# A fused attention, MLP and mixture-of-experts kernel: one more expert's first layer in fp32r, two loads moved, one wait dropped, new priorities

## The chip, the cores and the metric

The kernel runs on one core of a Trainium2 chip. A core has a matrix engine (TensorE, here PE, with a separate lane PEld for loading weights), three engines for element-wise work (VectorE: DVE, ScalarE: ACT, GpSimd: POOL), a SyncE (SP) that here only issues DMAs, and 16 DMA engines. Each engine runs its own list of instructions in order and waits on semaphores. The metric is the device time in microseconds (us) of one execution. Lower is better.

## The reference

Three layers, one behind the other, all in fp32 as seen from outside:

```python
# q, k, v: (2, 8, 768, 64); proj: (64, 6)
q_bits = np.einsum('bhsd,dk->bhsk', q, proj) > 0        # k_bits likewise
q_bucket = sum(q_bits * 2**arange(6))                    # k_bucket likewise
scores = where(q_bucket == k_bucket, q @ k.T / sqrt(64), -1e9)
x = softmax(scores) @ v                                  # -> (1536, 512)
x = maximum(x @ w_in, 0)**2 @ w_out                      # w_in (512, 2048)
logits = x @ w_gate                                      # 8 experts
for idx in argsort(-logits.flatten()):                   # greedy, best first
    tok, e = divmod(idx, 8)
    if not assigned[tok] and counts[e] < 192: assign(tok, e)
for e in range(8):                                       # w1 (512, 1024), w2 (1024, 512)
    out[mask[e]] = maximum(x[mask[e]] @ w1[e], 0) @ w2[e]
```

Every expert ends with exactly 192 tokens. Which token goes where depends on the order of all 12,288 logits.

## The kernel before

The kernel is written as a set of operations, each with an engine, a duration in a table, what it needs, the buffers it takes and gives back, and a priority. A small list scheduler (`Sched`) plays them through when the program is built and writes each engine's instructions in the order that comes out. On the chip that order is fixed; what varies is only how long each instruction waits. The priorities stand in tables: PREP, PREP1 and PR for attention, MP for the MLP, EP and RP for the router, FP for the experts. A change of a number there changes the order on all engines.

**Attention** has 16 heads, taken in pairs (0 to 7), and 96 units u of 128 queries. `first` prepares head 0 on its own: DVE and ACT copy the loaded k and q (L340, L342), PE transposes them (L355), ACT writes an upper part in fp32r (L360, L363), for q a second copy of it (L366), and DVE the lower part (L371, L374). PE then forms bucket bits (L384 and on). `second` does the same for head 1, `pair` for the later pairs; copies between SBUF partitions go by DMA from SP (L259, 14 for a pair). For each unit PE multiplies scores (L671), DVE takes the maximum (L687), ACT the exp (L690), POOL divides (L699), PE transposes the result (L707), ACT and DVE split it into upper and lower part (L715, L719) and PE multiplies it by v (L728, L729).

**The MLP** converts its weights on ACT and DVE (L870 to L878), splits them into upper and lower parts (ACT L884, POOL L886) and runs its first layer (L896) in the remaining gaps of attention and then by itself; the second layer is L923. The gate weights are loaded at L837, first thing after head 1's loads.

**The router** takes the logits of twelve token tiles. `early` compares all logits of a token (L1282 maximum, L1322 and L1343 comparisons on DVE), PE counts (L1362, L1364), and for each expert phase the router picks the next full expert and its tokens (L1453 comparisons, L1461 counts, and on to L1593, the token numbers). Its constants (`rck`) are loaded at L1148, ahead of everything else on SP, and read for the first time after attention. The routers of the later phases run beside the experts, on DVE above all.

**The experts** run in eight phases p, in the order that the router finds, each in four groups g of 256 hidden units. For a phase, SP reads the expert's number from SBUF and issues the weight loads of group 0 (L1739, L1740); POOL gathers the 192 token rows by two indirect DMAs (L1782) and then copies the number again (L1787), which lets SP issue the loads of groups 1 to 3; PE transposes the tokens (L1799), ACT and DVE bring them to SBUF (L1804, L1806, L1811, L1813). For p below `XP` the first layer is plain fp32 (L1893: eight multiplications of 192 columns a group), and ACT and DVE split the result into upper and lower part straight from PSUM (L1904, L1907). From `XP` on it runs in fp32r: the weights are split first (L1750 on ACT for the upper part, L1752 for the lower part, on POOL for even phases below 7), the upper weights are multiplied with both token parts side by side (L1851, 384 columns), the lower weights with the upper token part (L1852, 192 columns), and four steps form the result's two parts (L1860, L1863 on ACT, L1865, L1868 on DVE). The second layer is L1964 to L1971, its eviction L2027 to L2031, and POOL scatters the rows to the output (L2018).

Of the kernel before, what the change touches and what calls it, by code (L numbers as in the profile page):

```python
# [233 lines left out]
XC = -13  # L234
PREP, PW, DL = -224, 0.8, 2.4
PREP1 = 9.5
LDP = (2, 0)
PR = {"S": -6, "mx": 1033.5, "ex": 915, "dn": 242.5, "rec": -2168, "nrm": 581, "tp": -0.5, "hi": 240, "lo": -1372.5, "pv": 2, "oa": 1474, "od": 631.5, "pe": -246.5, "pa": 548.5, "pd": -695.5}

# [13 lines left out]
def attention(nc, S, ps, mem, ident, q, k, v, proj, pat, xhi, xlo):  # L253
# [9 lines left out]
    pf = mem(AT_PW + .5, [3, 32], R)  # L263
# [59 lines left out]
    def first(cm):  # L323
# [23 lines left out]
        def on(k):  # L347
            return "S" if k in FS else "B"
# [58 lines left out]
        for nm, hf in (("k", 0), ("q", 0), ("k", 1), ("q", 1)):  # L407
# [4 lines left out]
            if hf == 0:  # L412
                T["ci", nm, (0, 0)] = b
            c = add("ACT", .38, lambda hf=hf: hi2(hf), [a, b]) if nm == "q" else None
            d = add("DVE", .47, lambda nm=nm, hf=hf: lo(nm, hf), [a, b, c], rel=[(on("ft"), a)])
            H[nm, hf] = [x for x in (b, c, d) if x is not None]
        S.add("NONE", 0.0, None, [T["ft", "q", 1], T["ft", "k", 1]], rel=[("Pn", T["fl"])])
        out, o, early = [], None, None
        for x, hf in (("qk", 0), ("k", 1), ("q", 1)):
# [7 lines left out]
            if x == "k":  # L427
                early = list(out)
        return early, out

# [378 lines left out]
LEAST = 3.0517578125e-05  # L809
MP = {"lw": -1109, "ac": -526.5, "h1": 594, "h2": 869.5, "ch": -1952, "cv": 82, "sp": -784, "lg": -129, "ev": -2530, "lv": 292, "c0": 4755, "c1": 6377, "b0": -1565, "b1": 1274}  # L810


def mlp(nc, S, ps, mem, ident, xhi, xlo, w_in, w_out, w_gate, wgt, x2d, L, att):
# [22 lines left out]
    sw = S.add("NONE", 0.0, f1, last, rel=[(r, (3000 + u,)) for r, us in dict(r=(14,), xt=(35,)).items() for u in us])  # L836
    wgl = S.add("SP", .62, lambda: nc.sync.dma_start(wg, w_gate.rearrange("(c p) e -> p c e", p=128)), prio=MB)  # L837
    wgl = S.add("DMA", .1, None, [wgl], lat=1.8)
# [262 lines left out]

EP = {"fr": 1831, "lr": -1863.5, "row": -1595, "col": 240.5, "cp": 2055.5, "ca": 20, "gp": 1115}
LONE = 2
# [6 lines left out]
ND = 4  # L1110
RP = {"fr": 2209, "se": 1249, "oh": -1149, "G": 534, "A": -1001.5, "lr": -1816.5, "pf": -2980, "id": -1672, "gp": -626.5, "sq": 1082, "G1": -962, "A1": 813, "ei": -1561.5, "up": -1135.5}
ACT_TILES = {12: (10, 11), 9: (8,), 6: ()}
# [19 lines left out]
class Router:  # L1132
# [31 lines left out]

    def smalls(self, S, deps):
        k, P = self.k, self.nc.gpsimd
        alive, tok = self.alive, self.tok

# [919 lines left out]
def whole(tc, q, k, v, proj, w_in, w_out, w_gate, w1, w2, wgt, pat, rc, out):  # L2088
    nc = tc.nc
    with ExitStack() as ctx, tc.manual_schedule():  # L2090
# [58 lines left out]
```

## Time and profile before

| what | us |
| --- | --- |
| median of three timed runs | 759.81 (757.88 to 760.62) |
| the profiled execution | 757.53 |
| its span, first to last instruction | 755.7 |
| PE busy in the span | 740.3 (98%) |
| DVE busy | 562.8 (74%) |
| ACT busy | 454.9 (60%) |
| POOL busy | 328.5 (43%) |

The trace is one execution; its times count from the start of the span. A busy PE includes matmuls that overlap, so a sum of durations can be more than the time they took. In a row of the timeline, the bracket at the end is the idle time of that engine just before the instruction and what ended it. Attention lies from the start to about 240 us, the MLP up to about 540, the experts from about 560 to the end.

### The profile page before, as it was taken

The numbers are of one execution on the slowest core, as the hardware profiler recorded it, in microseconds if no ns is written. First come the engines' busy times: TensorE is split into PE (matmuls) and PEld (weight loads), VectorE is DVE, ScalarE is ACT, GpSimd is POOL, SyncE is SP. The second block draws the span as 40 slices with busy tenths as digits, with TensorE's granted clock in tenths as the row PEclk, the third lists the DMA queues.
The fourth block names the chain that finished last, engine by engine and source line by source line (L and its number), as shares of the span: only waits on it lengthen the run. The fifth ranks groups of instructions, "written<-read, shape, count | busy, mean of one in ns | idle before, by whom it ended". The sixth has DMA issues, their size and how long they took to land.

```text
span 755.7 us, 13988 instructions
## 1 busy us (share of the span) xinstructions
PE 740.3 (98%) x4955; PEld 652.8 (86%) x4955; DVE 562.8 (74%) x1213; ACT 454.9 (60%) x902; POOL 328.5 (43%) x362
## 2 busy tenths in 40 slices
PE   8999999999999999999999999999999999999996
PEld 5788988988988899998999999898768888888885
DVE  6899999999999876613853783236898978888883
ACT  7999999999998665533342433224453543345772
POOL 3788778778797775633100000004721121223521
PEclk9999999999999999999999999999899999999999
DMA  9879669575721122500330110021156467479921
GB/s 191 185 137 191 133 120 188 119 154 119 172 60 57 68 101 73 172 35 1 112 112 0 57 56 1 0 84 43 44 184 219 154 219 234 135 243 322 312 69 35
DMA packets 77109, 92.76 MB, mean 123 GB/s; under 512 B 29520, under 2 KB 56528, under 8 KB 77040
## 3 DMA queue, kind: packets, MB, share of 16 engines
q1 hardware_dynamic: 74992, 85.58, 41.5%
q0 software_dynamic: 2048, 6.29, 2.8%
q8 instruction: 39, 0.64, 0.4%
q14 instruction: 30, 0.25, 0.1%
HBM read 63.55 MB, written 6.29 MB: 92 GB/s over the span
## 4 chain that ended last, share of the span: by engine, by line
PE 76%; DVE 11%; ACT 4%; issue 3%; DMA 2%; POOL 2%; SPq 0%; POOLq 0%; ACTq 0%; DVEq 0%
PE psTP L896 17%; PE psS L923 12%; PE psS L1893 6%; DVE p L719 5%; PE psS L671 4%; PE psm L923 3%; PE psO L923 3%; DVE f L687 3%; PE psTP L707 2%; PE psO L707 2%; PE psS L1964 2%; PE psS L1968 2%; PE psS L1965 2%; PE psS L1971 2%; PE psS L1966 2%
## 5 line engine op out<-in xcount | busy, mean ns | idle before, releaser
L699 POOL TENSOR_TENSOR f<-f 128x768 f32<-128x768 f32 x96 | 141.7, 1478 | 24.8 <-PE psTP L707 7.9
L896 PE MATMUL psTP<-r 128*128 128x384 f32 x756 | 138.0, 336 | 0.0
L896 PEld LDWEIGHTS psTP<-r 128*128 128x128 f32 x756 | 132.3, 188 | 2.4 <-POOL r L886 0.2
L905 DVE TENSOR_TENSOR f<-f,psTP 128x384 f32<-128x384 f32 x63 | 34.9, 554 | 88.2 <-ACT f L903 88.1
L923 PE MATMUL psS<-r 128*128 128x512 f32 x384 | 100.3, 395 | 0.0
L687 DVE TENSOR_REDUCE f<-psS 128x1 f32<-128x768 f32 x96 | 90.6, 943 | 0.7 <-PE psS L671 0.5
L690 ACT ACTIVATE f<-psS,f 128x768 f32<-128x768 f32 x96 | 87.0, 906 | 5.4 <-POOL f L699 2.6
L671 PE MATMUL psS<-r 128*128 128x384 f32 x384 | 87.5, 349 | 1.7 <-ACT f L690 1.4
L903 ACT ACTIVATE f<-psTP 128x384 f32<-128x384 f32 x63 | 31.0, 492 | 86.0 <-PE psTP L896 85.9
L923 PEld LDWEIGHTS psS<-r 128*128 128x128 f32 x384 | 70.8, 188 | 12.7
L671 PEld LDWEIGHTS psS<-r 128*128 128x128 f32 x384 | 65.6, 188 | 5.3 <-ACT f L690 4.2
L1322 POOL TENSOR_SCALAR f<-f,mx 128x768 bf16<-128x768 f32 (+1 forms) x3 | 8.0, 2675 | 141.9 <-ACT f L1308 134.8
L1893 PE MATMUL psS<-ff,rf 128*128 128x192 f32 x320 | 60.4, 331 | 0.3 <-DVE ff L1813 0.3
L1750 ACT ACTIVATE ff<-rf 128x1024 fp32r<-128x1024 f32 x32 | 33.8, 1056 | 34.5 <-PE psS L1966 23.7
L1893 PEld LDWEIGHTS psS<-ff,rf 128*128 128x128 f32 x320 | 52.1, 190 | 2.4 <-DVE ff L1813 0.6
L907 ACT ACTIVATE r<-f 128x384 fp32r<-128x384 f32 x64 | 33.5, 524 | 32.0 <-DVE f L905 32.0
L2018 POOL DMA_INDIRECT out_dram<-ff,ix x16 | 17.6, 1102 | 80.6 <-DVE ff L2029 41.4
L719 DVE TENSOR_TENSOR p<-psTP,p 128x384 fp32r<-128x384 f32 x86 | 47.1, 549 | 5.4 <-ACT p L715 3.3
L909 POOL TENSOR_TENSOR r<-f,r 128x384 fp32r<-128x384 f32 x28 | 33.1, 1185 | 37.5 <-ACT r L907 29.2
L1782 POOL DMA_INDIRECT ff<-x2d,ix x16 | 18.2, 1137 | 66.1 <-DVE ix L1593 38.7
L728 PE MATMUL psTP<-p,r 128*128 128x384 f32 x114 | 46.4, 407 | 0.5 <-DVE p L719 0.5
L715 ACT ACTIVATE p<-psTP 128x384 fp32r<-128x384 f32 x86 | 42.4, 496 | 5.0 <-PE psTP L707 4.3
(422 smaller groups left out, 1797.9 us busy)
## 6 DMA issues: line engine op xcount, KB each, us to landing
rf<-in_moe_w_dram SPq DMA_DIRECT2D x64, 512.0 KB, 7.0
r<-r SPq DMA_DIRECT2D x84, 192.0 KB, 4.1
f<-in_moe_w_in_dram SPq DMA_DIRECT2D x16, 512.0 KB, 3.9
f<-in_moe_w_out_dram SPq DMA_DIRECT2D x16, 512.0 KB, 4.8
r<-r SPq DMA_DIRECT2D x14, 384.0 KB, 3.9
f<-in_k_dram SPq DMA_DIRECT2D x8, 384.0 KB, 6.4
f<-in_q_dram SPq DMA_DIRECT2D x8, 384.0 KB, 5.8
f<-in_v_dram SPq DMA_DIRECT2D x8, 384.0 KB, 4.8
```

Of the source, the lines that this page charges most:

```text
L671: nc.tensor.matmul(sbank(u)[:, hf, 0:384], T["q", (pr, h)][:, n, 128 * i:128 * i + 128], T["k", (pr, h)][:, n, 384 * hf:384 * hf + 384], s ...
L687: nc.vector.tensor_reduce(col(0, u), sbank(u)[:, :, 0:384], axis=AX.XY, op=OP.max, negate=True)
L690: nc.scalar.activation(P(u).rearrange("p (a b) -> p a b", a=2), sbank(u)[:, :, 0:384], AF.Exp, bias=col(0, u), accum_out=col(1, u))
L699: nc.gpsimd.tensor_tensor(Pn(u), P(u), col(3, u).to_broadcast([128, 768]), op=OP.mult)
L715: nc.scalar.activation(th, tp(u, g), AF.Copy)
L719: nc.vector.tensor_tensor(tl, tp(u, g), th.bitcast(F32), op=OP.subtract)
L728: nc.tensor.matmul(obank(g), w, th[:, c], start=(c == 0), stop=False)
L896: nc.tensor.matmul(hbank(s, hf), w[:, c], y[:, x, sl], start=(c == 0 and i == 0), stop=(c == 3 and i == 2))
L905: nc.vector.tensor_tensor(r, r, hbank(s, hf), op=OP.mult)
L923: nc.tensor.matmul(abank(i), a[:, t], w, start=(f == RUNS[r][1][0] and j == 0), stop=(f == RUNS[r][1][-1] and j == 2))
L1750: nc.scalar.activation(h(p, g, 0), w, AF.Copy)
L1893: nc.tensor.matmul(abank(n)[:, j], raw(p, g)[:, 0, 256 * c + 128 * j:256 * c + 128 * j + 128], xT(p)[:, c], start=(c == 0), stop=(c == 3))
```

## The change

Four things, in code that is otherwise the same. Line numbers grow by 3 from about L418 and by 5 from about L1170.

1. `XP` goes from 5 to 4: the fifth expert's first layer runs in fp32r too. Its phase is even, so its lower weight parts are formed on POOL.
2. The load of the router's constants moves from the start of the program into `smalls`, where it waits for the score matmul of unit 29 (`att[4][4]`); the load of the gate weights waits for that of unit 35 (`sos[5]`).
3. In `first`, the lower part of q no longer waits for q's second copy, which is now an operation of its own.
4. The priority tables have new numbers.

```diff
-PREP, PW, DL = -224, 0.8, 2.4
-PREP1 = 9.5
+PREP, PW, DL = -167, 0.8, 2.4
+PREP1 = 9
-PR = {"S": -6, "mx": 1033.5, "ex": 915, ...
+PR = {"S": -7, "mx": 1911, "ex": 835.5, ...
@@ first
-        ld, H = {}, {}
+        ld, H, H2 = {}, {}, []
...
-            c = add("ACT", .38, lambda hf=hf: hi2(hf), [a, b]) if nm == "q" else None
-            d = add("DVE", .47, lambda nm=nm, hf=hf: lo(nm, hf), [a, b, c], rel=[(on("ft"), a)])
-            H[nm, hf] = [x for x in (b, c, d) if x is not None]
+            d = add("DVE", .47, lambda nm=nm, hf=hf: lo(nm, hf), [a, b], rel=[(on("ft"), a)] if nm == "k" else ())
+            H[nm, hf] = [b, d]
+            if nm == "q":
+                c = S.add("ACT", .38, lambda hf=hf: hi2(hf), [a, b], prio=-99.5)
+                S.add("NONE", 0.0, None, [c, d], rel=[(on("ft"), a)])
+                H2.append(c)
...
-                early = list(out)
-        return early, out
+                early = [*out, H2[0]]
+        return early, [*out, *H2]
@@ mlp
-    wgl = S.add("SP", .62, lambda: nc.sync.dma_start(wg, ...), prio=MB)
+    wgl = S.add("SP", .62, lambda: nc.sync.dma_start(wg, ...), [sos[5]], prio=MB)
@@ Router
-        nc.sync.dma_start(k, rc)
+        self.rc = rc
...
+        a = S.add("SP", .62, lambda: self.nc.sync.dma_start(k, self.rc), begun, prio=MB)
+        deps = [*deps, S.add("DMA", .6, None, [a], lat=1.8)]
@@ experts
-HP, XP = 0, 5
+HP, XP = 0, 4
```

The order of the instructions, at the places where it matters. First SP at the start of the program; the names are the tile written and the tensor read. Before:

```order
L1148 DMA rck<-in_rc_dram 128x301
L334 DMA f_118<-in_k_dram 128x384
L334 DMA f_118<-in_q_dram 128x384
L275 DMA f_118<-in_proj_dram 64x6
L276 DMA f_118<-in_proj_dram 64x6
```

Now, the same place:

```order
L334 DMA f_117<-in_k_dram 128x384
L334 DMA f_117<-in_q_dram 128x384
L275 DMA f_117<-in_proj_dram 64x6
L276 DMA f_117<-in_proj_dram 64x6
L277 DMA f_117<-in_pat_dram 32x512
```

The two moved loads now stand some pairs further on, each among the copies (L259) that SP issues for a pair, the constants ahead of the last two copies of one pair and the gate weights within those of the next:

```order
L1170 DMA rck<-in_rc_dram 128x301
L259 DMA r_113<-r_113 64x768 x2
L538 DMA f_117<-in_v_dram 128x2x384
L540 DMA f_117<-in_q_dram 128x12x64
L540 DMA f_117<-in_k_dram 128x12x64
L259 DMA r_113<-r_113 64x2x768
L259 DMA r_113<-r_113 64x768
L840 DMA f_117<-in_moe_w_gate_dram 128x4x8
L259 DMA r_113<-r_113 64x768 x5
```

Five copies of that pair are behind the gate weights. Second, PE where the MLP's first matmuls (L896, now L899) enter attention; `p` are the split probabilities, `psS` the scores. Before:

```order
L728 MATMUL psTP_60<-p_122,r_114 128x384
L729 MATMUL psTP_60<-p_122,r_114 128x384
L707 MATMUL psO<-ident,f_118 128x128 x3
L671 MATMUL psS_71<-r_114 128x384 x4
L896 MATMUL psTP_61<-r_114 128x384 x9
L671 MATMUL psS_67<-r_114 128x384 x4
L896 MATMUL psTP_61<-r_114 128x384 x3
```

Now, the same place:

```order
L674 MATMUL psS_67<-r_113 128x384 x4
L731 MATMUL psO<-p_121,r_113 128x384
L732 MATMUL psO<-p_121,r_113 128x384
L899 MATMUL psm<-r_113 128x384 x3
L731 MATMUL psO<-p_121,r_113 128x384
L732 MATMUL psO<-p_121,r_113 128x384
L710 MATMUL psTP_61<-ident,f_117 128x128 x3
L674 MATMUL psS_71<-r_113 128x384 x4
```

The MLP's first pack of three now stands between probability matmuls, ahead of a score matmul that it stood behind. Third, POOL in the fifth expert (p = 4): two rows of the gather, the copy of the expert's number, the scatters of the expert before, the next gather. Before:

```order
L1782 DMA ff_5222<-x2d,ix 128x512
L1782 DMA ff_5222<-x2d,ix 64x512
L1787 COPY ei<-ei 128x1
L2017 MEMSET pad 128x1
L2018 DMA out_dram<-ff_5227,ix 1536x512
L2017 MEMSET pad 128x1
L2018 DMA out_dram<-ff_5228,ix 1536x512
L1782 DMA ff_5223<-x2d,ix 128x512
```

Now (the splits are L1757):

```order
L1787 DMA ff_5222<-x2d,ix 128x512
L1787 DMA ff_5222<-x2d,ix 64x512
L1757 TENSOR_TENSOR rf_5206<-rf_5204,rf_5206 128x1024
L1792 COPY ei<-ei 128x1
L1757 TENSOR_TENSOR rf_5207<-rf_5205,rf_5207 128x1024
L1787 DMA ff_5223<-x2d,ix 128x512
L1787 DMA ff_5223<-x2d,ix 64x512
L1792 COPY ei<-ei 128x1
L1757 TENSOR_TENSOR rf_5206<-rf_5197,rf_5206 128x1024
L2022 MEMSET pad 128x1
L2023 DMA out_dram<-ff_5227,ix 1536x512
```

Two splits now stand ahead of the next expert's gather, the first of them ahead of the copy that lets the loads of groups 1 to 3 go, and the scatters stand behind three of them.

## Rows read from the trace of the kernel before

**Rows 1.** The page: busy us, share of the span, instructions of each engine.

```profile
PE 740.3 (98%) x4955; PEld 652.8 (86%) x4955; DVE 562.8 (74%) x1213; ACT 454.9 (60%) x902; POOL 328.5 (43%) x362
```

**Rows 2.** Busy time by stretch: length, then busy us, PE clock, DMA share, GB/s.

```profile
core 0: us, PE busy (x) PEld busy (x) DVE busy (x) ACT busy (x) POOL busy (x), PEclk, DMA share, GB/s
0.00:40.00 40.00, 36.11 (x207) 27.23 (x208) 30.93 (x67) 34.64 (x80) 21.39 (x40) 1.00 0.94 190
...
200.00:240.00 40.00, 38.29 (x245) 33.82 (x244) 39.12 (x77) 36.59 (x80) 33.84 (x35) 1.00 0.31 75
240.00:280.00 40.00, 39.51 (x229) 36.68 (x229) 30.90 (x50) 28.75 (x56) 32.07 (x34) 1.00 0.24 82
...
720.00:760.00 40.00, 29.39 (x164) 24.88 (x162) 20.98 (x39) 17.25 (x37) 4.83 (x9) 0.96 0.09 29
```

**Rows 3.** Chain of waits, 0 to 16 us: start us, us, what.

```profile
0.74 0.40 SPq L1148
...
1.20 2.49 DMA f<-in_k_dram
...
6.39 0.38 ACT r L366
...
6.79 0.57 DVE r L374
...
7.41 0.99 PE psTP L384 x4
```

**Rows 4.** SP's timeline at the start; its waits, 61 to 91 us (total, times, longest).

```profile
9.07 1.73 SPq L837 DMA_DIRECT2D f<-in_moe_w_gate_dram  x1
...
SPq L259 <- ACT r L587: 6.1, 1, 6.1
```

**Rows 5.** PE's timeline where attention ends: start, us, instruction, [idle before <- releaser].

```profile
229.77 0.52 PE L707 MATMUL psTP<-ident,f 128*128 128x128 f32 x3 [0.35 <-DVE p L719]
...
236.19 0.55 PE L707 MATMUL psTP<-ident,f 128*128 128x128 f32 x3 [0.25 <-DVE p L719]
...
239.38 0.96 PE L671 MATMUL psS<-r 128*128 128x384 f32 x4 [0.80 <-ACT f L690]
```

**Rows 6.** DVE's timeline where the router's own steps begin.

```profile
544.33 0.17 DVE L1506 TENSOR_SCALAR full<-psS 128x8 f32<-128x8 f32 x1 [0.33 <-PE psS L1364]
```

**Rows 7.** PE's timeline, a group in fp32 and one in fp32r; all L1893.

```profile
606.37 2.85 PE L1893 MATMUL psS<-ff,rf 128*128 128x192 f32 x16
608.92 0.53 PE L1968 MATMUL psS<-ff,rf 128*128 128x512 f32 x1
...
694.50 0.33 PE L1851 MATMUL psS<-ff,rf 128*128 128x384 f32 x1
...
696.75 0.41 PE L1968 MATMUL psS<-ff,rf 128*128 128x512 f32 x1
...
L1893 PE MATMUL psS<-ff,rf x320: 323/326/430, 562.7 to 686.4; 128*128 128x192 f32 x160
```

**Rows 8.** Busy time by stretch, in the fifth expert and in the seventh.

```profile
660.00:680.00 20.00, 19.52 (x162) 17.17 (x161) 16.38 (x56) 7.92 (x12) 5.44 (x6) 1.00 0.75 249
...
700.00:720.00 20.00, 20.00 (x120) 17.83 (x120) 16.73 (x23) 15.05 (x31) 12.44 (x9) 1.00 0.97 330
```

**Rows 9.** POOL's and DVE's timelines in experts 5 to 8.

```profile
702.89 2.40 POOL L1752 TENSOR_TENSOR rf<-rf,rf 128x1024 fp32r<-128x1024 f32 x1 [1.96 <-ACT rf L1750]
703.05 2.72 DVE L1868 SCALAR_TENSOR_TENSOR rf<-rf,rf 128x128 fp32r<-128x128 f32 x2 [0.81 <-ACT rf L1860]
707.79 0.56 DVE L1806 TENSOR_TENSOR ff<-psm,ff 128x384 fp32r<-128x384 f32 x1 [0.35 <-ACT ff L1804]
708.73 1.62 DVE L1868 SCALAR_TENSOR_TENSOR rf<-rf,rf 128x128 fp32r<-128x128 f32 x2
...
723.53 0.61 DVE L1868 SCALAR_TENSOR_TENSOR rf<-rf,rf 128x128 fp32r<-128x128 f32 x2
744.25 0.36 DVE L1865 TENSOR_TENSOR rf<-psS,rf 128x192 f32<-128x192 f32 x1 [2.42 <-ACT rf L1860]
```

**Rows 10.** POOL's and SP's timelines as the fifth expert begins.

```profile
657.35 0.40 POOL L1787 COPY ei<-ei 128x1 int32<-128x1 int32 x1
...
658.56 0.37 SPq L1739 DMA_DIRECT2D rf<-in_moe_w_dram  x1
```

More of the change, by code (lines that the diff above doesn't have):

```diff
@@ L234 @@
 XC = -13
-PREP, PW, DL = -224, 0.8, 2.4
-PREP1 = 9.5
+PREP, PW, DL = -167, 0.8, 2.4
+PREP1 = 9
 LDP = (2, 0)
-PR = {"S": -6, "mx": 1033.5, "ex": 915, "dn": 242.5, "rec": -2168, "nrm": 581, "tp": -0.5, "hi": 240, "lo": -1372.5, "pv": 2, "oa": 1474, "od": 631.5, "pe": -246.5, "pa": 548.5, "pd": -695.5}
+PR = {"S": -7, "mx": 1911, "ex": 835.5, "dn": 546.5, "rec": -1981.5, "nrm": 371, "tp": -1.5, "hi": 125, "lo": -1316, "pv": 1, "oa": 2110.5, "od": 863.5, "pe": -190.5, "pa": 640.5, "pd": -370.5}
 def host_consts_a():
@@ L809 @@
 LEAST = 3.0517578125e-05
-MP = {"lw": -1109, "ac": -526.5, "h1": 594, "h2": 869.5, "ch": -1952, "cv": 82, "sp": -784, "lg": -129, "ev": -2530, "lv": 292, "c0": 4755, "c1": 6377, "b0": -1565, "b1": 1274}
+MP = {"lw": -951, "ac": 558.5, "h1": 786.5, "h2": 808, "ch": -1545.5, "cv": 485, "sp": -1044.5, "lg": 723.5, "ev": -3211.5, "lv": 292, "c0": 5307, "c1": 6736, "b0": -3040, "b1": 556}
 def mlp(nc, S, ps, mem, ident, xhi, xlo, w_in, w_out, w_gate, wgt, x2d, L, att):
@@ L836, in mlp @@
     sw = S.add("NONE", 0.0, f1, last, rel=[(r, (3000 + u,)) for r, us in dict(r=(14,), xt=(35,)).items() for u in us])
-    wgl = S.add("SP", .62, lambda: nc.sync.dma_start(wg, w_gate.rearrange("(c p) e -> p c e", p=128)), prio=MB)
+    wgl = S.add("SP", .62, lambda: nc.sync.dma_start(wg, w_gate.rearrange("(c p) e -> p c e", p=128)), [sos[5]], prio=MB)
     wgl = S.add("DMA", .1, None, [wgl], lat=1.8)
@@ L1099, in mlp @@
     return [ld[n] for n in range(12)], st, [i for f in range(16) for i in Wd[f]], []
-EP = {"fr": 1831, "lr": -1863.5, "row": -1595, "col": 240.5, "cp": 2055.5, "ca": 20, "gp": 1115}
+EP = {"fr": 518, "lr": -2926.5, "row": -3002.5, "col": 3034.5, "cp": 130, "ca": -426.5, "gp": 1965}
 LONE = 2
@@ L1110 @@
 ND = 4
-RP = {"fr": 2209, "se": 1249, "oh": -1149, "G": 534, "A": -1001.5, "lr": -1816.5, "pf": -2980, "id": -1672, "gp": -626.5, "sq": 1082, "G1": -962, "A1": 813, "ei": -1561.5, "up": -1135.5}
+RP = {"fr": 3870.5, "se": 672, "oh": -906.5, "G": -856, "A": -1016, "lr": -615.5, "pf": -4061.5, "id": -2189, "gp": -43, "sq": 543, "G1": -466.5, "A1": 1392, "ei": -1672, "up": -292}
 ACT_TILES = {12: (10, 11), 9: (8,), 6: ()}
@@ L1163, in slot, with smalls @@
         return self.mem(self.SLOT, [128, 12], F16)
-    def smalls(self, S, deps):
+    def smalls(self, S, deps, begun):
         k, P = self.k, self.nc.gpsimd
+        a = S.add("SP", .62, lambda: self.nc.sync.dma_start(k, self.rc), begun, prio=MB)
+        deps = [*deps, S.add("DMA", .6, None, [a], lat=1.8)]
         alive, tok = self.alive, self.tok
@@ L1697, in squeeze @@
         st["L"], st["alive"], st["tok"] = a, None, e1
-FP = {"s1": -1161.5, "ga": -1309.5, "xp": 816.5, "xe": -655, "m1": 866, "re": -351.5, "m2": 104, "ye": -956, "yt": 335, "yo": -2032, "sc": -2225, "sp": -162.5, "mr": 866}
+FP = {"s1": -648, "ga": -655, "xp": 542, "xe": -1283.5, "m1": 892.5, "re": -59, "m2": 104, "ye": -956, "yt": 335, "yo": -2705, "sc": -3178.5, "sp": -36, "mr": 892.5}
 AP = 5
-HP, XP = 0, 5
+HP, XP = 0, 4
 RSLACK, ESLACK = 0, 0.2
@@ L2106, in whole @@
         L, st, free, dots = mlp(nc, S, ps, mem, ident, xhi, xlo, w_in.bitcast(I32), w_out.bitcast(I32), w_gate, wgt, x2d, router.L, att)
-        cst = router.smalls(S, [i for e in att[0] for i in e])
+        cst = router.smalls(S, [i for e in att[0] for i in e], [att[4][4]])
         S.slack = ESLACK
```

## The prediction, made before the changed kernel ran

> **What bounds the kernel now.** First the busy line of the page, which says TensorE (PE) is at work 98% of the span [rows 1]: 755.7 - 740.3 leaves 15.4 us in which it is not. Then the table of busy time by stretch, to place these 15.4 us [rows 2]. The first 40 us hold 40 - 36.11 = 3.9 of them, the last, cut off at 755.7, hold 35.7 - 29.39 = 6.3 (a tail of evictions and scatters whose order the change leaves alone), and 200 to 280 us, where attention hands over to the MLP, hold 1.71 + 0.49 = 2.2. What is left, some 3.0 us, is strewn. So no reordering can give more than the 3.9 + 2.2 + 3.0 of visible idle, and of the 3.9 most is the fixed wait for the first data. Anything else must come out of PE's own work. Third, the chain of waits at the start and the PE timeline at the handover, for what ends each idle stretch there [rows 3, 5]. Last, the stretches of the late experts, for how much room VectorE (DVE) has in the place where the new work falls [rows 8, 9].
>
> **The sum, part by part.** All durations are of the one profiled execution (757.53 us, its span 755.7). The median of the three timed runs is 759.81, so that execution is 2.3 us on the fast side; I work out a difference and put it on the median.
>
> *The start.* Before, the queue on SyncE (SP) issues the load of the routing constants first, at 0.74 us, and the first key load starts at 1.20 [rows 3]. With the constants gone the key load is first: 1.20 - 0.74 = 0.46 us off the chain that starts everything. Then DVE's lower part of q (L374) waits for both ACT copies: the second (L366, 0.38 us in the chain) stands between, and PE's L384 waits for L374 [rows 3]. The change drops that wait, so up to 0.38 us more. The second half of the head goes through the same engines once again and ACT's work there is not shorter, so I take 0.3. Together -0.75 us; the ends are -0.46 (only the issue) and -0.84. That PE is the bound from some 40 us on carries the whole of it to the end.
>
> *The two moved loads.* They cost SP 1.73 us (gate weights, L837, before at 9.07) and 0.40 us (constants) [rows 3, 4], now some pairs further on, among the 14 copies of a pair. Behind the gate load stand five of the copies for the next heads; whoever needs these waits up to 1.73 us longer if nothing hides it. What hides it is the queue's own idle time: in the pair that I looked at, its longest single wait (for ACT's L587) is 6.1 us [rows 4], more than both loads, and PE has no wait for a copy there. I put it at 0; without the cover it is +1.7, once. The constants are read by the router alone, and most of attention still lies between.
>
> *Attention to MLP.* PE waits 0.35 and 0.25 us for DVE's L719 and 0.80 us for ACT's exp (L690), just ahead of the first nine MLP matmuls [rows 5]. In the new order MLP matmuls in packs of three stand between the last heads' PV matmuls, before the score matmul that waited, and PE has something to do in these gaps. All three gone is 0.35 + 0.25 + 0.80 = 1.40 us, and I take it whole. One end is the whole visible idle of these 80 us, -2.2 [rows 2]. The other is +0.3: the new order lets DVE's weight conversions follow each other more closely, and a gap as long as the shorter ones of today may open elsewhere.
>
> *MLP to router.* DVE does the same instructions in another order, the two long ones of the last token tiles (L1343) now behind all short ones. The wait of PE's counts on the last short one goes; the 0.33 us that DVE then waits for the counts [rows 6] can shrink. I take -0.25, ends -0.33 and +0.4 (as much lost as there was to be gained).
>
> *Expert 4's first layer on PE* (phases count from 0: the fifth expert is 4, the seventh 6). In fp32, a group takes from 606.37 to 608.92, 2.55 us; in fp32r from 694.50 to 696.75, 2.25 us [rows 7]. Four groups: 4 x 0.30 = -1.2 us. PE is the bound there (20.00 of 20 us busy, or close [rows 8]), so this one is real unless PE waits for something new.
>
> *What that costs on DVE and POOL.* Expert 4 now needs the lower halves of its first weights: four splits on GpSimd (POOL) at 2.40 us [rows 9], where POOL now has almost nothing to do. On DVE each group gets two additions (L1865, 0.36) and the pair L1868 (0.61) for a pair L1907 that I count as equal; the transposed tokens add one eviction (0.56) [rows 9]. That is 4 x 0.72 + 0.56 = 3.4 us. DVE is busy 16.38 of 20 us there [rows 8], so an expert takes 24.7 us (five fp32 ones from 562.7 to 686.4 [rows 7]), and in that time it has 24.7 x 3.62 / 20 = 4.5 us to spare: 1.1 us are left. And the splits hold DVE up: the pair L1868 takes 0.61 us alone, but 2.72 beside a POOL split, and 1.62 where it meets the end of one [rows 9]. That is 1.0 to 2.1 us for a split. Expert 6 has the same splits today, and while DVE loses those microseconds PE stays at 20.00 of 20 [rows 8]; but in expert 4 the router for the experts behind it still runs on DVE, and PE waits for its results. So the cost lies between 0 (as in expert 6) and 4 x 2.1 - 1.1 = 7.3 us (every microsecond beyond the spare ones reaches PE). Against the upper end speaks that in the new order the router's steps stand about a group earlier against PE. I take a quarter, +1.8.
>
> The rule of the Trainium skill that speaks against this edit is in "SBUF — State Buffer", section "Who interferes with whom": VectorE and GpSimd share a port pair that one instruction holds for its whole length, and a VectorE operation with two SBUF inputs is shut out by a GpSimd operation that reads SBUF. The trace agrees: 2.72 us beside 0.61, and the PSUM-fed L1806 kept its 0.56 us during a split [rows 9]. By the rule taken alone each of the four splits could cost DVE its whole 2.40 us.
>
> Sum: -0.75 - 1.4 - 0.25 - 1.2 + 1.8 = -1.8 us. On the median: 759.81 - 1.8 = **758.0 us** (on the profiled execution 755.7).
>
> **Rivals.**
> *A, DVE becomes the bound in expert 4 (the other side).* Place: the last 25 us before 686.4. Price: the 7.3 us above in place of 1.8. It decides once the splits take more than the 1.1 us that DVE has to spare and the router's lead of a group does not absorb it; as soon as one router step of experts 5 and 6 comes late, PE, which has all its work in one order, stands still. For it: the 2.72 us rows; against it: PE's 20.00 in 700 to 720. Time: 759.81 - 3.6 + 7.3 = 763.5.
> *B, late weights.* POOL's copy L1787 (the expert's number for the later loads) ran at 657.35, and the loads of groups 1 to 3 followed at 658.56 [rows 10]. Now the first split stands between gather and copy, so those loads start at least 2.40 us later, plus what the split itself waits for. Group 1 is due one group after group 0, some 6 us. For it: no other wait in the change has a DMA behind it; against it: weights come early now, and the free buffers may have been the limit. About 3 us once: 761.0.
> *C, everything fits.* The handover's 2.2 us go whole, the start gives 0.84, the router 0.33, and nothing is lost in expert 4: 759.81 - 0.84 - 2.2 - 0.33 - 1.2 = 755.2.
> *D, only the start remains.* The gap at the handover moves and the matmuls saved in expert 4 are waited away: about 759.1.
> *E, the change doesn't do what it says.* The instruction order shows the fp32r forms in expert 4 and the loads at their new places; I give it nothing. It would be 759.8.
>
> **How the numbers follow.** Forecast 0.43 (758.0), A 0.11, B 0.12, C 0.22, D 0.12. About 0.5% (3.8 us) is what a measurement of this kernel can tell from no change: below 756.0 is faster, above 763.6 slower. C is faster, and a small part of the forecast's own spread (the terms' ends reach -3.6 before any cost): 0.27. Slower is the far part of A, with a little for what I do not see: 0.08. The rest, 0.65, is within 0.5%. The range goes from 754.5, a little below C, to 761.5, above B; A's upper part, and a C with more than the named gaps, stay outside.
>
> **What would show each step.** Start: the first key load issued near 0.74, PE's first L384 some 0.8 us earlier. Handover: PE's busy time in 200 to 240 at 39.5 or more, and no wait of 0.80 for exp before the first MLP matmuls. Expert 4: groups of 2.25 us with fp32r forms, POOL splits of 2.40, pairs of the old L1868 over 1.5 us long, and PE's idle time in 655 to 690: under 2 us by the forecast, 5 or more by A with DVE as releaser, some 3 with ACT's split or a DMA as releaser by B. I am wrong if PE's idle time between 40 and 200 us grows (a copy late behind the gate load), or if steady attention itself got shorter by the new priorities: PE is full there, and I see nothing to take.

## The result, and the profile after

The changed kernel takes **763.92 us** (763.14 to 764.45); the kernel before, beside it, 759.07. The ratio is 1.0064, 95% interval 1.0051 to 1.0077: slower by 4.9 us, where 758.0 was forecast with a range up to 761.5. Rival A, VectorE held up in expert 4, had given 763.5.

The profiled execution took 764.41 us, its span 762.6. The page of the changed kernel, its busy line (to hold against [rows 1]), and its busy time by stretch (against [rows 2, 8]; length, busy us of each engine, PE clock, DMA share, GB/s):

```profile
PE 744.2 (98%) x4954; PEld 654.0 (86%) x4954; DVE 572.5 (75%) x1222; ACT 461.1 (60%) x919; POOL 340.0 (45%) x366
...
220.00:240.00 20.00, 17.66 (x103) 14.06 (x100) 19.70 (x34) 16.61 (x35) 17.13 (x15) 1.00 0.16 54
...
640.00:660.00 20.00, 17.92 (x141) 15.38 (x140) 16.66 (x53) 7.36 (x11) 6.94 (x7) 0.91 0.39 123
660.00:680.00 20.00, 18.66 (x148) 15.84 (x147) 15.88 (x53) 8.67 (x16) 6.29 (x5) 0.91 0.71 237
```

PE's share is the same 98%, yet its busy time has grown by 3.9 us although it was given less to do. That is the first sign that the clock has part in it: at a lower clock PE is busy for longer with the same work, and 640 to 680 us is the place where the clock is no longer 1.00.

Where the 6.9 us between the two spans arose is read from the same instruction in both traces (row maxima on DVE for units of attention, the first step L1506, now L1511, for the router):

| instruction | before | after | difference |
| --- | --- | --- | --- |
| row maximum, unit 0 | 13.66 | 13.55 | -0.11 |
| row maximum, unit 30 | 86.23 | 86.24 | +0.01 |
| row maximum, unit 48 | 131.21 | 131.95 | +0.74 |
| row maximum, unit 78 | 205.10 | 206.06 | +0.96 |
| router's own steps begin | 544.33 | 545.51 | +1.18 |
| end of the span | 755.7 | 762.6 | +6.9 |

So 5.7 us are lost behind the router's start, some 0.9 in attention, and the start and the handover have given nothing. What PE waits for from 640 to 690 us, in the view of waits of the changed kernel (us in total, times, longest):

```profile
PE psTP L1466 <- DVE ff L1458: 2.1, 2, 1.9
PE psTP L1594 <- DVE ff L1588: 1.3, 1, 1.3
PE psm L1256 <- DVE mm L1544: 0.3, 1, 0.3
```

In the same window of the kernel before there is one such wait, and none for the router:

```profile
PE psTP L1799 <- DMA ff<-x2d,ix: 0.4, 1, 0.4
```

And the place itself, from the timelines of POOL, DVE and PE, before and in the changed kernel (start, us, instruction, [idle before <- releaser]; L1458 are the router's comparisons, L1466 its counts, L1757 the splits, L1898 expert 3's fp32 first layer; the two rows of the kernel before are the last two comparisons of the same count, and that count):

```profile
656.45 1.26 DVE L1453 TENSOR_SCALAR ff<-ff,mx 128x768 bf16<-128x768 f32 x2
657.98 0.46 PE L1461 MATMUL psO<-Bb,ff 128*128 128x8 bf16 x12
```

After:

```profile
653.24 2.39 POOL L1757 TENSOR_TENSOR rf<-rf,rf 128x1024 fp32r<-128x1024 f32 x1
653.30 3.29 DVE L1458 TENSOR_SCALAR ff<-ff,mx 128x768 bf16<-128x768 f32 x2 [0.86 <-PE psTP L1466]
656.11 0.30 PE L1466 MATMUL psTP<-Bb,ff 128*128 128x8 bf16 x6 [1.85 <-DVE ff L1458]
656.83 2.91 PE L1898 MATMUL psS<-ff,rf 128*128 128x192 f32 x8
659.73 1.47 PE L1898 MATMUL psS<-ff,rf 128*128 128x192 f32 x8
...
667.93 2.38 POOL L1757 TENSOR_TENSOR rf<-rf,rf 128x1024 fp32r<-128x1024 f32 x1 [11.83 <-ACT rf L1755]
668.16 2.57 DVE L1458 TENSOR_SCALAR ff<-ff,mx 128x768 bf16<-128x768 f32 x1 [0.17 <-ACT ff L1432]
671.32 0.44 PE L1594 MATMUL psTP<-mv,ff 128*128 128x2 f16 x6 [1.34 <-DVE ff L1588]
```

Read from the top: before, two comparisons take 1.26 us and PE's counts follow without a wait. After, a split begins on POOL at 653.24; the two comparisons that DVE begins at 653.30 last 3.29 us, the first until 0.42 us behind the split's end, the second the usual 0.6 us longer; PE, which needs their results for its counts, idles 1.85 us; and the eight matmuls behind that take 2.91 us, the next eight, alike, 1.47. The same once more at 667.93. The busy time by stretch says why the 2.91, in its clock column (the first row is the kernel before, the others the changed one):

```profile
656.00:660.00 4.00, 4.00 (x60) 3.46 (x59) 3.28 (x12) 1.06 (x1) 1.48 (x4) 1.00 0.40 113
...
656.00:660.00 4.00, 3.66 (x23) 3.39 (x24) 2.55 (x9) 0.00 (x0) 0.10 (x1) 0.57 0.48 149
...
672.00:676.00 4.00, 4.00 (x42) 3.38 (x40) 3.88 (x9) 1.06 (x1) 2.88 (x3) 0.67 0.29 81
676.00:680.00 4.00, 4.00 (x21) 3.37 (x20) 2.03 (x9) 2.83 (x7) 1.03 (x1) 0.90 0.63 200
```

Behind each of the two waits the granted clock falls from 2.4 to 1.2 GHz (1.00 to 0.50) for part of the stretch, which gives the means of 0.57, 0.67 and 0.90: 4 x 0.43 + 4 x 0.33 + 4 x 0.10 = 3.4 us of PE's work. With PE's waits of 3.7 us, less the 1.2 saved in the first layer and the wait of some 0.4 that was there before, that is 5.5 of the 5.7 us in this one execution.

### The profile page after: what moved, and what is told of

The parts are those of the page before. It is cut to its first block, busy times and chain, and to the rows that moved or that the text cites. A ratio compares the mean times of both kernels' runs of the same rounds, so it can differ in the third digit from the quotient of the medians.

```text
span 762.6 us, 14037 instructions
## 1 busy us (share of the span) xinstructions
PE 744.2 (98%) x4954; PEld 654.0 (86%) x4954; DVE 572.5 (75%) x1222; ACT 461.1 (60%) x919; POOL 340.0 (45%) x366
## 4 chain that ended last, share of the span: by engine, by line
PE 76%; DVE 12%; ACT 4%; issue 4%; POOL 2%; DMA 0%; SPq 0%; POOLq 0%; ACTq 0%; DVEq 0%
PE psTP L899 17%; PE psS L926 12%; PE psS L1898 6%; PE psS L674 4%; DVE p L722 4%; DVE f L690 3%; PE psm L926 3%; PE psO L926 3%; PE psTP L710 2%; PE psS L1973 2%; PE psS L1969 2%; PE psTP L731 2%; PE psS L1970 1%; PE psS L1971 1%; PE psS L1976 1%
## 5 line engine op out<-in xcount | busy, mean ns | idle before, releaser
L899 PE MATMUL psTP<-r 128*128 128x384 f32 x756 | 137.9, 336 | 0.0
L899 PEld LDWEIGHTS psTP<-r 128*128 128x128 f32 x756 | 132.3, 188 | 2.2
L926 PE MATMUL psS<-r 128*128 128x512 f32 x384 | 96.2, 394 | 0.0
L1755 ACT ACTIVATE ff<-rf 128x1024 fp32r<-128x1024 f32 x32 | 33.8, 1056 | 39.1 <-PE psS L1971 31.3
L722 DVE TENSOR_TENSOR p<-psTP,p 128x384 fp32r<-128x384 f32 x96 | 51.9, 547 | 5.0 <-ACT p L718 4.3
L1898 PE MATMUL psS<-ff,rf 128*128 128x192 f32 x256 | 50.6, 339 | 0.3 <-DVE ff L1818 0.3
L718 ACT ACTIVATE p<-psTP 128x384 fp32r<-128x384 f32 x96 | 46.9, 498 | 5.0 <-PE psTP L710 3.9
L710 PE MATMUL psTP<-ident,f 128*128 128x128 f32 x288 | 47.7, 275 | 1.2 <-DVE p L722 1.0
L1898 PEld LDWEIGHTS psS<-ff,rf 128*128 128x128 f32 x256 | 42.6, 195 | 1.7 <-DVE ff L1818 0.6
L1757 DVE TENSOR_TENSOR ff<-rf,ff 128x1024 fp32r<-128x1024 f32 x32 | 39.0, 1220 | 5.5 <-ACT ff L1755 5.2
```

Source lines behind the costliest of these rows:

```text
L710: nc.tensor.transpose(tp(u, g)[:, j], Pn(u)[:, 128 * c:128 * c + 128], ident)
L718: nc.scalar.activation(th, tp(u, g), AF.Copy)
L722: nc.vector.tensor_tensor(tl, tp(u, g), th.bitcast(F32), op=OP.subtract)
L899: nc.tensor.matmul(hbank(s, hf), w[:, c], y[:, x, sl], start=(c == 0 and i == 0), stop=(c == 3 and i == 2))
L926: nc.tensor.matmul(abank(i), a[:, t], w, start=(f == RUNS[r][1][0] and j == 0), stop=(f == RUNS[r][1][-1] and j == 2))
L1757: e.tensor_tensor(h(p, g, 1), w, h(p, g, 0).bitcast(F32), op=OP.subtract)
```

## The experiments

**Is it the port, VectorE's load, or the late weights?** Four kernels. In the first every engine keeps its order and only the engine of four instructions changes:

```diff
-... lambda: split(1, 0, w1h, nc.gpsimd if on == "POOL" else nc.vector), ...
+... lambda: split(1, 0, w1h, nc.gpsimd if on == "POOL" and p != 4 else nc.vector), ...
```

> The changed kernel with the order of every engine kept; only expert 4's four lower-half splits go to VectorE at the places where the plan had them, instead of GpSimd. Theory L (a GpSimd split holds VectorE's comparisons, PE then idles and its clock falls): the two comparisons that took 3.29 us take about 1.2 again, PE's wait of 1.85 us before the counts goes, the granted clock stays at 1.00 there; but VectorE gets 4 x 1.24 us more, so 759.5 to 761.5 in place of 763.9. Rival W (VectorE simply has too much work in expert 4, the port plays no part): 5 us more of it makes it worse, 764 to 768. Rival B (weights of groups 1 to 3 come late, since the number's copy waits for a split on GpSimd): gains about 1 to 2 us, and the comparisons' durations have nothing to do with it.

Measured: 759.02 us, ratio to before 1.0005 (0.9995 to 1.0015). DVE has 5 us more to do, and the kernel is 4.5 us faster than the changed one (1.0064 less 1.0005, of 758.5). DVE's and PE's timelines and one stretch in this kernel:

```profile
654.06 1.15 DVE L1458 TENSOR_SCALAR ff<-ff,mx 128x768 bf16<-128x768 f32 x2 [1.68 <-PE psTP L1466]
...
654.74 0.30 PE L1466 MATMUL psTP<-Bb,ff 128*128 128x8 bf16 x6 [0.53 <-DVE ff L1458]
...
655.43 1.55 PE L1898 MATMUL psS<-ff,rf 128*128 128x192 f32 x8
...
656.00:660.00 4.00, 3.88 (x28) 3.39 (x27) 3.44 (x14) 1.23 (x3) 0.00 (x0) 1.00 0.84 274
```

The comparisons take 1.15 us, the wait is 0.53, the clock stays 1.00, from 645 to 690 us too. Rival W (VectorE's load) falls: it predicted a loss. Rival B (late weights) had 1 to 2 us for this, and no row in which PE waits for a DMA or for a split of the weights in this stretch of the changed kernel; it falls too.

In the second the splits aren't done at all, and the upper weights stand in for the lower ones:

```diff
-W1[p, g] = S.add(on, ..., lambda: split(1, 0, w1h, ...), [a], ...)
+W1[p, g] = S.add(on, ..., (lambda: split(1, 0, w1h, ...)) if p != 4 else None, [a], ...)
-hi, lo = (w1h(p, g, i)[...] for i in range(2))
+hi, lo = (w1h(p, g, 0 if p == 4 else i)[...] for i in range(2))
```

> The changed kernel with the order of every engine kept, but expert 4's lower weight halves are not formed at all: the upper halves are multiplied twice, so this part of the result is left out. Theory L: neither GpSimd nor VectorE spends time on the splits, PE has no wait over 0.5 us from 645 to 690 us and no lowered clock there; 757.5 to 759.5. Rival W (the 3.4 us of added additions and evictions on VectorE overload it): 761.5 to 763.5, with PE still waiting for VectorE.

Measured: 757.92 us, 0.9986 (0.9975 to 0.9997). From 645 to 690 us PE waits 0.52 and 0.23 us, both times for the comparisons, and the clock stays at 1.00. All additions and evictions of the change are still on DVE, so these cost next to nothing; the four splits on DVE cost 1.1 us by the medians (1.4 by the ratios), on POOL 5.9.

The third takes expert 4 back to fp32 and leaves the rest of the change (`XP = 5`); the planner orders it anew.

> The changed kernel with expert 4's first layer back in fp32; everything else of the change stays, the planner makes a new order. Theory L (nearly all of the loss is in expert 4): 758.5 to 760.5. Rival P (the new priorities lose the time, in attention and in the router): 762 or more.

Measured: 758.72 us, 1.0006 (0.9996 to 1.0016). All else in the change together gives or costs nothing that can be told from zero (the interval is -0.3 to +1.2 us); what the fp32r step costs is 1.0064 less 1.0006, 4.4 us.

The fourth does that step alone, in the kernel before (`XP = 4`).

> The kernel before with expert 4's first layer in fp32r and nothing else, planned anew with the old priorities. Theory L: slower than before by 2 to 6 us, 761 to 765, with comparisons on VectorE of over 1 us each beside a GpSimd split. Rival P (the new priorities are what loses): 757.5 to 759, the 1.2 us of PE's work saved.

Measured: 769.02 us, 1.0129 (1.0101 to 1.0157). Worse than the 2 to 6 us expected. Timelines of DVE, POOL and PE in this kernel (its line numbers are those of before):

```profile
656.73 3.59 DVE L1453 TENSOR_SCALAR ff<-ff,mx 128x768 bf16<-128x768 f32 x2
...
672.18 2.37 DVE L1577 TENSOR_TENSOR mv<-tok,mv 128x6 f16<-128x6 f16 x1
...
686.41 4.66 POOL L1752 TENSOR_TENSOR rf<-rf,rf 128x1024 fp32r<-128x1024 f32 x2
688.82 0.53 PE L1852 MATMUL psS<-ff,rf 128*128 128x192 f32 x1 [4.67 <-POOL rf L1752]
```

The same hold-up, even of an operation on six columns (2.37 us), and a second one: POOL, which works in order, has put two splits behind a scatter and a gather, and PE waits 4.67 us for them. The changed kernel has no such wait: with the change's priorities the same step costs 4.9 us less (1.0129 less 1.0064).

**The clock.** 48 multiplications by a zero tile fill the wait at 654 us.

```diff
+        zero6 = lambda d, R: [nc.tensor.matmul(R[:, 0:8 * n], self.zero, self.zero[:, 0:8 * n], ...) for _ in range(48 if ... else 0)]
...
-                done.append(k)
+                done.append(k); zero6(len(done), T["R"]) if n == 6 else None
```

> The changed kernel with 48 multiplications by a zero tile put on PE just ahead of the counts that wait 1.85 us at 654 to 656 us; they add zero to the same sum. Every other engine is as in the changed kernel, and VectorE's comparisons still take over 3 us beside the GpSimd split. Theory C (about 1.7 us of the loss is the lower clock behind that wait, 0.57 from 656 to 660): the clock stays at 1.00 there and the time falls to 761.8 to 762.6. Rival: the clock falls in spite of it or the fill costs as much as it saves, 763.5 to 764.5.

PE's and DVE's timelines and the stretch behind:

```profile
653.42 4.00 DVE L1458 TENSOR_SCALAR ff<-ff,mx 128x768 bf16<-128x768 f32 x2 [0.17 <-PE psTP L1466]
...
654.92 1.37 PE L1469 MATMUL psTP<-zero 128*128 128x48 bf16 x48
656.95 0.30 PE L1466 MATMUL psTP<-Bb,ff 128*128 128x8 bf16 x6 [0.65 <-DVE ff L1458]
...
656.00:660.00 4.00, 3.12 (x39) 2.85 (x36) 3.50 (x9) 0.22 (x1) 0.93 (x2) 1.00 0.29 83
```

The hold-up is there as before, the clock now stays at 1.00, and from the start of the counting (L1436) to expert 4's first transpose (L1804) it takes 660.54 - 652.90 = 7.64 us in place of 661.14 - 652.08 = 9.06: in the changed kernel the lower clock behind this one wait costs 1.4 us. The whole run is 764.06 us, 1.0067 (1.0041 to 1.0094), the rival's time and not the theory's. In this execution the clock fell again at the second wait (672 us), which has no fill, and at a place where the changed kernel's execution kept 1.00. The rows from 556 to 560 us, first of the changed kernel, then of this one:

```profile
556.00:560.00 4.00, 3.56 (x72) 2.46 (x70) 4.00 (x5) 3.97 (x4) 3.69 (x3) 1.00 0.24 66
...
556.00:560.00 4.00, 3.57 (x53) 2.00 (x50) 4.00 (x5) 3.97 (x4) 3.59 (x3) 0.62 0.21 66
```

That took back most of what the first wait had kept. Nor is it shown that the fill kept the clock up: the next kernel has a longer wait there, no fill, and a clock of 1.00.

**Shorter instructions on POOL.** Each split in four pieces of 256 columns.

```diff
-e.tensor_tensor(h(p, g, 1), w, h(p, g, 0)..., op=OP.subtract)
+[e.tensor_tensor(h(p, g, 1)[:, s:s + m], w[:, s:s + m], h(p, g, 0)[:, s:s + m]..., op=OP.subtract)
+ for m in (256 if p == 4 and e is nc.gpsimd else 1024,) for s in range(0, 1024, m)]
```

> The changed kernel with every order kept, but each of expert 4's four splits on GpSimd made of four pieces of 256 columns. Theory L (a VectorE operation is shut out until the GpSimd instruction in progress ends, so shorter instructions let it in between): the two comparisons take 1.8 to 2.6 us in place of 3.29, PE's wait before the counts falls to under 1.2 us and the clock behind it stays nearer to 1.00; 760 to 762.5. Rival (GpSimd's next piece takes the port again before VectorE gets it): 3.2 us or more, 763.5 to 764.5.

Measured: 763.96 us, 1.0077 (1.006 to 1.0095). Theory L failed; the rival had 3.2 us or more and 763.5 to 764.5. Timelines of DVE, POOL and PE, and two stretches:

```profile
652.58 4.39 DVE L1458 TENSOR_SCALAR ff<-ff,mx 128x768 bf16<-128x768 f32 x2 [0.17 <-PE psTP L1466]
653.23 2.79 POOL L1757 TENSOR_TENSOR rf<-rf,rf 128x256 fp32r<-128x256 f32 x4
656.50 0.30 PE L1466 MATMUL psTP<-Bb,ff 128*128 128x8 bf16 x6 [2.25 <-DVE ff L1458]
...
656.00:660.00 4.00, 3.28 (x30) 3.09 (x31) 3.05 (x9) 0.00 (x0) 0.48 (x2) 1.00 0.36 114
672.00:676.00 4.00, 4.00 (x31) 3.77 (x28) 3.34 (x11) 0.99 (x3) 2.35 (x3) 0.57 0.38 102
```

The comparison is held until the last of the four pieces is over (653.23 + 2.79 = 656.02). At the second split DVE did get in between: the four pieces took 3.83 us, and in place of PE's one wait of 1.34 there are three, of 0.25, 0.41 and 0.29. So pieces back to back are no sure way out. The clock follows neither wait by its length: it stays at 1.00 behind the 2.25 us and falls behind the three short ones. What holds over the runs is less: in all four kernels with expert 4's splits on POOL it fell at least once between 650 and 690 us of the profiled execution, in the other ten never.

**The 0.7 us in attention.** I took them first for the copies behind the moved gate load. The gate load goes back, ahead of the first load of v, in the kernel of the first experiment:

```diff
-wgl = S.add("SP", .62, lambda: nc.sync.dma_start(wg, ...), [sos[5]], prio=MB)
+LATER.append(lambda: nc.sync.dma_start(wg, ...)); wgl = S.add("SP", .62, None, [sos[5]], prio=MB)
...
+LATER and LATER.pop()()
```

> The kernel of e1 (759.0 us) with every engine's order kept, only the load of the gate weights goes back to its old place on SyncE, behind the first heads' loads. Theory G (behind the moved load, the copies for the heads of the fourth pair come late; the traces put that at about 0.7 us between units 24 and 48): the row maximum of unit 48 comes 0.6 to 0.8 us earlier against the kernel before than in the changed kernel (+0.74 there), and the whole is 758.2 to 758.5. Rival P (the new priorities lose those 0.7 us themselves): no change there, 759.0.

Measured: 757.81 us, 0.9995 (0.9984 to 1.0006); this interval and the one of the kernel without the edit (0.9995 to 1.0015) overlap. In the trace unit 24 stands at -0.35 and unit 48 at +0.37 against before: the same step of 0.7. The theory fell. What it leaves is the order that the planner made. The load of the constants, alone, in the kernel before:

```diff
-        nc.sync.dma_start(k, rc)
+        a = S.add("SP", .62, lambda: self.nc.sync.dma_start(k, self.rc), begun, prio=MB)
```

> The kernel before with only the load of the routing constants moved as the change has it, planned anew: by the order this moves PE's work between the third and the fifth pair, and nothing behind it. Theory K (it is this new order, with PE's transposes and scores standing without a probability matmul between them, that loses 0.7 us between units 36 and 48): row maximum of unit 12 at -0.1 to -0.4 against before, unit 48 at +0.3 to +0.7; whole run +0.2 to +0.6. Rival (the loss needs the other parts of the change too): unit 48 at -0.4 to 0, whole run -0.4.

Unit 12 stands at -0.73 against before, unit 30 at -0.75, unit 48 at 0.00: the step of 0.7 us, with no other part of the change there. By its absolute numbers the expectation missed, and the rival's unit 48 and whole run came. What Theory K had too small is the gain at the start, 0.75 us in this execution (its scatter is in the last section); that the loss needs the other parts, as the rival says, the step contradicts. In PE's timeline of this kernel the step begins here:

```profile
107.79 0.52 PE L707 MATMUL psO<-ident,f 128*128 128x128 f32 x3 [0.35 <-DVE p L719]
```

In the changed kernel, at the same instruction in its order:

```profile
108.51 0.52 PE L710 MATMUL psTP<-ident,f 128*128 128x128 f32 x3 [0.35 <-DVE p L722]
```

The whole run: 757.54 us, 0.9991 (0.9981 to 1.0002), not to be told from before. The planner, which counts 0.62 us on SP for the load, makes a new order on PE from 96 us on, and the new order waits for DVE: PE's idle time from 84 to 135 us is 0.55 us in place of 0.13. The rest of the step was not traced.

**The start.** In the kernel of the first experiment the second copy of q's first half comes two places later on ACT:

```diff
+b = add("ACT", .38, lambda ...: (hi(nm, hf), hi2(0) if (nm, hf) == ("q", 1) else None), ...)
-c = S.add("ACT", .38, lambda hf=hf: hi2(hf), [a, b], prio=-99.5)
+c = S.add("ACT", .38, lambda hf=hf: hi2(hf) if hf else None, [a, b], prio=-99.5)
```

> The kernel of e1 (759.0 us) with the second copy of q's first half (L366) moved on ScalarE behind the next two copies, everything else in the same order. Theory S (in the changed kernel the lower part of q, L374, still waits for that copy in the program, though the planner no longer asks for it): the lower part starts right behind L363, about 5.9 us in place of 6.27, PE's first L384 some 0.35 us earlier, and the first row maximum 0.1 to 0.3 us earlier; 758.7 to 759.0. Rival: the lower part starts at 6.27 as before, because something else holds it.

Measured: 757.56 us, 0.9994 (0.9982 to 1.0005), unit 0 at 12.59 (-1.07 against before; -0.01 without the edit). The rows are below, beside those of the changed kernel. The whole run's interval overlaps that of the kernel without the edit, and not all of the 1.06 us is the edit's: in this execution PE's first transposes had reached double speed by 4.5 us (last section). The same edit and the constants' load behind the first loads, in the kernel before, all other orders kept:

> The kernel before with two things alone: the load of the routing constants stands on SyncE behind the first loads and the gate weights, and on ScalarE the second copy of q's first half comes behind the next two copies. No other engine's order moves. Theory S (the start gives 0.46 us by the load and some 0.3 to 0.6 by the copy, and PE being full from 40 us on carries it to the end): all units 0.8 to 1.1 us earlier, 756.7 to 757.4 with before at 757.9. Rival: the start is taken up again by later waits, within 0.3 us of before.

Measured: **756.79 us, 0.998 (0.997 to 0.9989)**: faster than before by 1.0 us (medians), with every unit 0.93 to 0.97 us earlier, from unit 0 to unit 95. This is the best version found, and better than both kernels. How the 1.0 us divides between load and copy the runs don't tell: the load alone, with a new order, had an interval of 0.9981 to 1.0002.

**The handover.** The new attention tables alone, in the kernel before:

> The kernel before with the change's attention tables alone (PREP, PREP1, PR), planned anew: the order differs only from about unit 84 on, where attention hands over to the MLP. Theory H (at the handover the waits only change places: DVE's parts of the probabilities end last in the new order too): PE waits 0.3 to 0.9 us for DVE three or four times from 225 to 240, and the router starts within 0.6 us of before, to either side; 757.5 to 758.5. Rival (forecast): 1.4 us faster, 756.5.

Measured: 762.06 us, 1.0045 (1.003 to 1.0061), slower by 3.4 us and worse than either theory. PE's waits in this kernel from 222 to 262 us:

```profile
PE psO L707 <- DVE p L719: 2.1, 1, 2.1
PE psTP L728 <- DVE p L719: 0.9, 1, 0.9
```

The 2.1 us come on top of waits that the changed kernel has there too (0.9, 0.7, 0.6 and 0.2); behind them the clock falls, to a mean of 0.64 from 256 to 260 us. The profiled execution, 763.61 us, was the slowest of five, and 2.06 us of it were lost by unit 0, where the order of all engines is still that of before (last section). The attention tables lose by themselves; with the rest of the change (the third kernel above) nothing was lost.

**All three repairs, planned anew.** The planner is told that expert 4's splits go to VectorE, and the gate load and the second copy are moved as above.

> The changed kernel with expert 4's four splits on VectorE known to the planner (a new order), the gate load at its old place and the second copy of q late. If the three losses are all there is, 757.0 to 758.3, a little below before (758.5); if VectorE has too little room once the planner packs it, 759 to 761.

Measured: 778.78 us, 1.0264 (1.0241 to 1.0286). The new order puts the expert number's copy in expert 6 behind a gather, a split and a scatter on POOL; the weights' loads stop for 16 us. SP's timeline and PE's waits from 690 to 750 us:

```profile
700.26 0.37 SPq L1745 DMA_DIRECT2D rf<-in_moe_w_dram  x1
716.87 0.37 SPq L1744 DMA_DIRECT2D rf<-in_moe_w_dram  x1
...
PE psS L1973 <- DVE rf L1873: 8.6, 3, 3.9
PE psS L1857 <- POOL rf L1757: 2.0, 1, 2.0
```

PE's releasers in these rows are DVE and POOL, which follow the late loads: ACT's split L1755 waits for a load at 720.75 for 2.26 us. This is what Rival B had described, in another expert. It doesn't say that the three repairs are bad; with the order kept, each was harmless.

## Why the prediction was wrong, by its steps

**Expert 4, the term that failed.** The sum had -1.2 for PE's matmuls and +1.8 for splits and DVE. With splits left out the fp32r layer gains 758.72 - 757.92 = 0.8 us against fp32 (1.5 by the ratios), not far from 1.2, so this term stands. With the splits on POOL the whole step costs 4.4; the +1.8 should have been some 5.2 to 5.9. The mechanism was named and priced (Rival A: 7.3, time 763.5 against 763.9), and then I took a quarter of it, by the row in which PE stays at 20.00 of 20 us in expert 6 [rows 8]. That row was the wrong neighbour, and the text itself said why: in expert 6 nobody on PE waits for what DVE is held in, in expert 4 the router's chain is exactly that. Beyond this three things were sized wrongly:
- What is held. I counted four hold-ups of L1868 (1.0 to 2.1 us each). Those that cost were two hold-ups of the router's comparisons, of 2.1 us (3.29 in place of 1.15 for two) and of 2.0 (2.57 in place of about 0.6 for one). The pairs of L1868 (now L1873) were held at the other two splits, and PE had no wait for them.
- The lead. "The router's steps stand about a group earlier" was read from the order, and an order says nothing of the time that lies between two instructions. PE reached the counts 1.85 us before their inputs.
- The clock. No term of the sum had it. Of the 6.8 us lost at these two places 3.4 are PE's lower clock behind the waits.

The Trainium skill, "SBUF — State Buffer", section "Who interferes with whom", gives the lock for a VectorE operation in a two-port mode and, against a GpSimd operation that reads SBUF, for one with two SBUF inputs; it counts `tensor_scalar` among those that can enter such a mode. The trace agrees for the comparison, a TENSOR_SCALAR (3.29 us beside 1.15), which I had not counted among the operations in danger; which mode it ran in no trace shows.

**The start, -0.75.** Given: -0.11 at unit 0 in this pair of executions; over the seven with this start unit 0 lies between 13.12 and 13.65, over the three with the start of before at 13.66, 13.98 and 15.72. The load's 0.46 came: PE's first L384 began at 6.88 in place of 7.41 [rows 3]. The dropped wait didn't. ACT, DVE and PE in the changed kernel:

```profile
5.76 0.47 ACT L366 ACTIVATE r<-psm 64x384 fp32r<-64x384 f32 x1
6.27 0.56 DVE L374 SCALAR_TENSOR_TENSOR r<-psm,r 64x384 fp32r<-64x384 f32 x1 [0.46 <-ACT r L366]
6.88 1.38 PE L384 MATMUL psTP<-r 128*32 128x384 f32 x4 [0.26 <-DVE r L374]
```

DVE's L374 still begins just when L366 is over. The edit takes the wait from the planner, and the program has kept it: L366 still stands ahead of L374, and both write into the same tile. With L366 two places later (the kernel of the experiment):

```profile
5.70 0.56 DVE L374 SCALAR_TENSOR_TENSOR r<-psm,r 64x384 fp32r<-64x384 f32 x1
6.32 0.99 PE L384 MATMUL psTP<-r 128*32 128x384 f32 x4 [0.77 <-DVE r L374]
```

L374 begins behind DVE's own preceding instruction. In the kernel of all three repairs, with the same edit and transposes as slow as in the changed kernel, it begins at 5.90, and L384 at 6.52: the wait is worth 0.36 us, near the 0.3 that the prediction took. So Rival E, to which I gave nothing, was true of this part: I had read the wait in the plan, and ACT's order there is the same in both traces. The rest of the lost start is L384 itself, 1.38 us in place of 0.99; see the last section.

**The moved loads, 0.** The gate load cost nothing that can be told, as forecast. The constants' load cost 0.7 us in the trace, by the new order on PE and not by SP's time. The prediction had asked only what waits behind the loads on SP, and had no term for a new order of PE in steady attention. Its list of what would prove it wrong had PE's idle time between 40 and 200 us, which grew from 0.30 to 0.74, though for DVE and not for the late copy that it named.

**The handover, -1.4.** PE's timeline of the changed kernel there, for [rows 5]:

```profile
228.93 0.55 PE L710 MATMUL psTP<-ident,f 128*128 128x128 f32 x3 [0.67 <-DVE p L722]
233.08 0.96 PE L674 MATMUL psS<-r 128*128 128x384 f32 x4 [0.19 <-ACT f L693]
234.61 0.55 PE L710 MATMUL psO<-ident,f 128*128 128x128 f32 x3 [0.57 <-DVE p L722]
237.02 0.41 PE L731 MATMUL psO<-p,r 128*128 128x384 f32 x1 [0.85 <-DVE p L722]
```

The waits of 0.35, 0.25 and 0.80 are gone and four others have come, 2.28 us. DVE is at work for 19.70 of the 20 us there: the work that PE lacks is what DVE hasn't finished. That filling one gap with MLP matmuls only brings PE sooner to the next is my reading of these rows. PE's busy time from 200 to 240, which was to be 39.5 or more, is 37.66 us, less than the 38.29 of before. Unit 78 stands at +0.96, the router at +1.18; with the -0.25 that was forecast for the router's start, nothing of 1.65 us came. What the router's change of order gave by itself was not tried.

The range failed because its upper end left out Rival A on the ground of the quarter; the chance of 0.11 for A was too low for a mechanism that three rows of the profile showed. That A's 763.5 lies so near the measured 763.92 is luck: it takes 7.3 us for splits and DVE, which measured 5.2 to 5.9, and beside them 2.4 us of gains from start, handover and router, which didn't come, on a base (759.81) that was 0.7 us above the median measured beside the changed kernel. Its own sign, 5 us or more of PE idle between 655 and 690, was not met either: 3.1 us, released by DVE, and the rest is the clock. And the sentence that the terms' ends reach -3.6 is a slip: -3.6 is the sum of the terms taken, the ends reach -4.6.

## What to carry to other kernels

Before work is given to GpSimd because it stands idle, list what VectorE does in that stretch and who waits for it: if TensorE waits on the same chain, count every split as a full hold-up, and leave room for what the clock may take behind TensorE's wait. Here that was some 1.4 to 1.7 us each time, and it can't be told from the wait's length: the clock fell behind 1.85 and 1.34 us of idling and not behind 2.25 in the kernel with split pieces. Take a neighbour in the trace as evidence only if the waiting engine depends on the held one in both places. A wait dropped from a planner's model need not be gone from the program (here it went when the order of ScalarE changed), and a load moved in the model can change orders far from the load; compare the order of every engine first, and move instructions by hand, with all else kept, to see what each is worth.

## What the runs showed of the hardware beyond this

Four short GpSimd instructions back to back held one VectorE comparison until the last was over (656.02; 4.39 us for two comparisons), though at another place VectorE came in between. In three traces (the changed kernel, the zero tile, the pieces) the held comparison ends 0.42 or 0.43 us behind the end of the last split instruction. In the latter two it had begun 0.65 us ahead of the split, longer than the 0.61 it takes alone, so having begun first did not free it; POOL was at the gather's DMA then, and what held it until the split the traces don't say.

In the first microseconds PE's matmuls double their speed at a moment that differs from run to run: three transposes (L355) take 0.85 us and later 0.49, with the change between 4.3 and 4.7 us in three runs, past 6 us in the kernel before, past 7 in the changed kernel and past 12 in the kernel with the attention tables alone, while the clock column shows 1.00 throughout. Kernels with the changed kernel's first instructions had unit 0 between 13.12 (splits in quarters) and 13.65 (splits on VectorE), those with the first instructions of before between 13.66 and 15.72. What sets the moment was not tried; it is why a start gained or lost by less than 0.5 us, with the start of before even by 2 us, isn't seen in a single profile.
